# Attention block on one core: the VectorE share of the exponentials by rows of four heads as bit fields and two products, instead of single tiles by a cubic in half precision

## The chip, the cores and the metric

The kernel runs on one core of a Trainium2 chip. The metric is the device time of one execution in microseconds; a measurement is the median of several runs. The core has five engines that run side by side, each through its own list of instructions in order: TensorE (PE, with its weight loads shown apart as PEld), ScalarE (ACT), VectorE (DVE), GpSimd (POOL) and SyncE (SP, which here only starts DMAs). They meet through semaphores. Working memory is SBUF; TensorE writes to PSUM, which has eight banks of 512 fp32 values in each of 128 partitions.

## The reference

One block of multi-head attention, B = 1, S = 2048, D = 448, 16 heads of Dh = 28, all in bf16:

```python
qkv = (x @ wqkv).reshape(B, S, 3, H, Dh).transpose(2, 0, 3, 1, 4)
q, k, v = qkv[0], qkv[1], qkv[2]
scores = jnp.einsum("bhqd,bhkd->bhqk", q, k) * (Dh ** -0.5)
p = softmax(scores, axis=-1)
o = jnp.einsum("bhqk,bhkd->bhqd", p, v)
return o.transpose(0, 2, 1, 3).reshape(B, S, D) @ wo
```

The exponentials are the bulk: 16 x 2048 x 2048 of them. No maximum is subtracted; the row sum is carried by a column of ones in V (column 28 of each head's 32).

## The kernel before

**Tiles and units.** The scores are held transposed: keys on the 128 partitions, 512 queries along the bank. A tile is one head, 128 keys, 512 queries, so one bank. A unit is a group of four heads and a chunk of 512 queries; there are 16 units, and each has 16 key blocks (`kt`) of four tiles, one for each head: 64 tiles a unit, 1024 in all. Below, a *row* is the four tiles of one unit and one `kt`. Scores come out multiplied by 128/ln 2, since Q is scaled so, and ScalarE divides again in its `scale`.

**Two engines take exponentials.** Most tiles go to ScalarE: TensorE writes the scores of a group of tiles to neighbouring banks (line 874, four heads at four row positions of the array, which run side by side), and one ACTIVATE (line 897) turns the whole group into bf16 in `PT`. In unit 0 two groups of two banks take turns (banks 0-1 and 2-3), after it two groups of three (banks 0-2 and 3-5). The other 135 tiles, which a table (`PLAN["tiles"]`) names one by one, go to VectorE through a bank of their own. There, line 919 clips a tile out of PSUM into fp32 `DT`; then two tiles together, 1024 wide, go through lines 931, 933, 935, 937 and 939: a scale of the low 16 bits into fp16, a square, an addition, a product, and a last instruction that adds the polynomial to the fp32 value and rounds it to the 16 bits of a bf16.

**P times V.** For each row, line 830 multiplies the four tiles by V, four heads at four column positions, into one PSUM bank that collects the 16 rows of a unit. This waits for the slowest of the four tiles.

**The rest.** Unit 0 also holds the transposes of x (line 543) and the first projections (560, 577); the other projections of K, Q and V are spread through later units as jobs whose results VectorE moves out of PSUM (lines 529, 531). After a unit, VectorE copies the sum out (line 737), the row sums travel through DRAM to be spread over partitions, and line 753 multiplies by their reciprocals. The last four units also carry the output projection (724, 712). At the end of the last unit a short chain finishes the last 512 queries.

**Banks.** Banks 6 and 7 form the pool "M": the open sum of P times V has one, and the VectorE scores, the projection jobs and the output projection share the other.

**The order.** It is written by a planner in the kernel itself. Each operation has a length, a priority and what it depends on; a list schedule (`schedule`) gives every engine its fixed order. Where TensorE would have too little to do, it inserts passes over zeros (line 479, four matmuls each) that add nothing to an open bank. On the chip an engine that comes to an instruction whose operands aren't there stands, and with it all that is behind it in its list.

The functions follow with the lines of the profile.

Of the kernel before, what the change touches and what calls it, by code (L numbers as in the profile page):

```python
# [7 lines left out]
ALU = mybir.AluOpType  # L8
# [54 lines left out]
class _Prog:  # L63
# [278 lines left out]
PLAN = {
    "tiles": [32, 39, 46, 48, 58, 59, 81, 89, 90, 99, 107, 112, 115, 119, 138, 141, 149, 165, 166, 178, 182, 191, 193, 209, 218, 220, 226, 227, 230, 246, 
# [4 lines left out]
    "late": [0.807, 1.353, 1.300, 1.475, 1.303, 2.070, 1.710, 2.020, 2.419, 2.615, 3.120, 3.693, 4.014, 4.168, 3.895, 4.140, 4.490, 4.389, 4.691, 5.132,   # L348
    5.193, 5.700, 5.935, 5.720, 6.151, 6.521, 6.730, 6.828, 6.866, 6.891, 7.366, 7.749, 7.826, 8.270, 8.397, 8.737, 8.874, 9.279],
# [3 lines left out]
def _fast(nc, x, wqkv, wo, out, n_heads=16):  # L353
# [16 lines left out]
    NPD = 10  # L370
    NDB = 3
# [16 lines left out]
    with es:  # L388
# [3 lines left out]
        x_nat = sb("x_nat", [128, NST, D], BF16)  # L392
# [7 lines left out]
        PD = sb("PD", [128, NPD * 512], I16)  # L400
        DT = sb("DT", [128, NDB, 1024], FP32)
        DW = sb("DW", [128, NDB, 1024], FP16)
        DU = sb("DU", [128, NDB, 1024], FP16)
        OTS = sb("OTS", [128, 2, 512], FP32)
        RS = sb("RS", [128, NU * 16], FP32)
        OTN = sb("OTN", [128, G, S], BF16)
# [1303 lines left out]
```

## Time and profile before

| | |
|---|---|
| median of 3 runs | 418.77 us (418.65 to 418.83) |
| span of the profiled execution | 416.9 us |
| ACT busy | 402.2 us, 96%, 311 instructions |
| DVE busy | 380.1 us, 91%, 615 instructions |
| PE busy | 384.9 us, 92%, 4568 matmuls, of them 1556 over zeros |
| POOL busy | 3.4 us, 9 instructions, all in the first microseconds |
| granted TensorE clock | 1.000 |

The profiled execution is 1.9 us shorter than the median of the runs, since its span goes only from the first to the last instruction. A row of a group gives the line in the code, the engine, the operation with the tile it writes and the tile it reads, their sizes, the count, then the busy time in us and the mean ns of one, and last the idle time before them with what ended it. Busy times of a group are a union: where instructions overlap, the busy time is less than count times mean. The cadence (from one start to the next) is then the better price of an instruction, and it is read from the timeline or from the chain of waits.

### The profile page before, as it was taken

The page shows a single profiled execution, that of the slowest core. Times are in us where ns is not written, and L with a number is a line of the kernel's source. Part 1 is how long each engine was busy: PE and PEld are TensorE (multiplying, and loading weights), DVE is VectorE, ACT ScalarE, POOL GpSimd, SP SyncE. Part 2 cuts the span into 40 slices and gives each one's busy share as a digit, 9 for nine tenths or more (in the row PEclk, how much of TensorE's full clock was granted, in tenths as well). Part 3 has the DMA queues.
Part 4 walks back from the last instruction along what each step waited for, and adds up shares of the span by engine and source line. Part 5 has one row for each costly group of instructions (what it writes and reads, how often), then busy time and mean ns, then how long its engine had stood idle before and what let it go on. Part 6 is the DMA issues. An engine that isn't in the chain of part 4 may idle for free.

```text
span 416.9 us, 10252 instructions
## 1 busy us (share of the span) xinstructions
PE 384.9 (92%) x4568; PEld 122.2 (29%) x4568; DVE 380.1 (91%) x615; ACT 402.2 (96%) x311; POOL 3.4 (1%) x9
## 2 busy tenths in 40 slices
PE   8999989999999999998899899898988999899996
PEld 3432222323332232232232222322223322222223
DVE  6699989999798999999999999999999789999934
ACT  2999999999999999999999999999999999999993
POOL 3000000000000000000000000000000000000000
PEclk9999999999999999999999999999999999999999
DMA  8200000000000000000000000000000000010111
GB/s 264 68 2 3 24 6 7 24 3 28 2 5 27 3 26 2 28 2 8 23 3 30 2 28 2 7 25 3 28 2 28 2 4 27 14 38 24 54 55 57
DMA packets 12982, 10.29 MB, mean 25 GB/s; under 512 B 5064, under 2 KB 10952, under 8 KB 12932
## 3 DMA queue, kind: packets, MB, share of 16 engines
q1 hardware_dynamic: 12132, 8.92, 6.9%
q8 instruction: 37, 0.61, 0.6%
q10 hardware_dynamic: 800, 0.66, 0.5%
q14 instruction: 13, 0.11, 0.1%
HBM read 7.50 MB, written 2.08 MB: 23 GB/s over the span
## 4 chain that ended last, share of the span: by engine, by line
ACT 83%; DVE 7%; DMA 5%; PE 3%; issue 1%; SPq 0%; ACTq 0%
ACT PT L897 83%; DMA RB<-scr_r 2%; DVE DT L919 2%; DMA scr_r<-RS 2%; DMA w_raw<-in_wqkv_dram 1%; DVE PD L939 1%; PE ps L874 1%; DVE DW L931 1%; DVE DU L937 1%; DVE DU L933 1%; PE ps L772 1%; PE ps L830 1%; DVE OTN L753 0%; PE ps L724 0%; DVE OUTS L712 0%
## 5 line engine op out<-in xcount | busy, mean ns | idle before, releaser
L897 ACT ACTIVATE PT<-ps 128x1536 bf16<-128x1536 f32 (+1 forms) x307 | 399.2, 1763 | 1.3 <-PE ps L874 1.0
L874 PE MATMUL ps<-QT,KT 28*128 28x512 bf16 x1024 | 153.2, 384 | 22.9 <-ACT PT L897 18.5
L479 PE MATMUL ps<-ZM,ZW 128*32 128x512 bf16 x1556 | 121.7, 385 | 1.2 <-DVE ZM L461 1.2
L919 DVE TENSOR_SCALAR DT<-ps 128x512 f32<-128x512 f32 x135 | 92.3, 686 | 8.8 <-PE ps L874 8.3
L830 PE MATMUL ps<-PT,V 128*32 128x512 bf16 x889 | 96.1, 388 | 2.6 <-DVE OTS L737 1.0
L874 PEld LDWEIGHTS ps<-QT,KT 28*128 28x128 bf16 x1024 | 36.3, 91 | 157.9 <-ACT PT L897 123.1
L939 DVE SCALAR_TENSOR_TENSOR PD<-DT,DU 128x1024 int16<-128x1024 f32 x68 | 81.9, 1204 | 0.3
L479 PEld LDWEIGHTS ps<-ZM,ZW 128*32 128x32 bf16 x1556 | 37.8, 96 | 39.0 <-issue 20.7
L931 DVE TENSOR_SCALAR DW<-DT 128x1024 f16<-128x1024 uint16 x68 | 46.5, 684 | 0.6
L937 DVE TENSOR_TENSOR DU<-DU,DW 128x1024 f16<-128x1024 f16 x68 | 46.4, 682 | 0.7
L933 DVE TENSOR_TENSOR DU<-DW 128x1024 f16<-128x1024 f16 x68 | 46.3, 681 | 0.6
L830 PE MATMUL ps<-PD,V 128*32 128x512 bf16 x135 | 43.2, 387 | 0.3 <-DVE PD L939 0.2
L830 PEld LDWEIGHTS ps<-PT,V 128*32 128x32 bf16 x889 | 23.7, 93 | 54.9 <-issue 43.6
L560 PE MATMUL ps<-xT,w_raw 112*32 112x512 bf16 x512 | 34.5, 381 | 0.6 <-DMA w_raw<-in_wqkv_dram 0.4
L935 DVE TENSOR_SCALAR DU<-DU 128x1024 f16<-128x1024 f16 x68 | 28.4, 418 | 0.5
L577 PE MATMUL ps<-w_raw,xT 112*128 112x112 bf16 x256 | 16.6, 214 | 0.0
L560 PEld LDWEIGHTS ps<-xT,w_raw 112*32 112x32 bf16 x512 | 11.6, 95 | 14.3 <-issue 2.5
L577 PEld LDWEIGHTS ps<-w_raw,xT 112*128 112x128 bf16 x256 | 13.0, 98 | 5.2 <-issue 4.5
L712 DVE CAST OUTS<-ps 128x448 bf16<-128x448 f32 x14 | 8.5, 622 | 6.0 <-PE ps L724 3.5
L531 DVE CAST KT<-ps 128x512 bf16<-128x512 f32 x16 | 11.0, 687 | 3.2 <-PE ps L560 3.0
L753 DVE TENSOR_TENSOR OTN<-RB,OTS 128x512 bf16<-128x512 f32 x15 | 10.3, 685 | 3.2 <-DMA RB<-scr_r 3.2
L830 PEld LDWEIGHTS ps<-PD,V 128*32 128x32 bf16 x135 | 10.2, 93 | 8.2 <-issue 6.6
(46 smaller groups left out, 94.4 us busy)
## 6 DMA issues: line engine op xcount, KB each, us to landing
RB<-scr_r SPq DMA_DIRECT2D x15, 256.0 KB
out_dram<-OUTS SPq DMA_DIRECT2D x14, 112.0 KB, 1.7
x_nat<-in_x_dram SPq DMA_DIRECT2D x3, 448.0 KB, 7.3
w_raw<-in_wqkv_dram SPq DMA_DIRECT2D x2, 392.0 KB, 6.7
wop<-in_wo_dram SPq DMA_DIRECT2D x16, 24.5 KB
scr_l<-OTS SPq DMA_DIRECT2D x15, 8.0 KB
LT<-scr_l SPq DMA_DIRECT2D x15, 8.0 KB, 1.6
scr_r<-RS SPq DMA_DIRECT2D x15, 8.0 KB, 1.4
```

Source lines behind the costliest of these rows:

```text
L479: ins = e.matmul(ps[32 * h:32 * h + 32, b * 512:(b + 1) * 512], ZW[:, :], ZM[:, :], start=shut, stop=shut, skip_group_check=not shut, tile ...
L560: ins = e.matmul(ps[32 * h:32 * h + 32, b * 512:(b + 1) * 512], w_raw[0:IT, it, col:col + 32], xT[0:IT, it, c * 512:(c + 1) * 512], start= ...
L577: ins = e.matmul(ps[:, b * 512 + j * GD:b * 512 + (j + 1) * GD], xT[0:IT, it, n * 128:(n + 1) * 128], w_raw[0:IT, it, 2 * D + g * GD:2 * D ...
L830: ins = e.matmul(ps[32 * h:32 * h + 32, b * 512:(b + 1) * 512], V[:, kt, hh * 32:(hh + 1) * 32], p_ap, start=(kt == 0), stop=(kt == NK - 1 ...
L874: ins = e.matmul(bank(b), KT[32 * h:32 * h + rows, g, kt * 128:(kt + 1) * 128], QT[32 * h:32 * h + rows, g, c * QCH:(c + 1) * QCH], start= ...
L897: ex = P.add("act", (lambda e, p0=p0, w=w, bf=bf: e.activation(PT[:, p0 * 512:(p0 + w) * 512], bank(bf(), w), AF.Exp, scale=ESCALE)), deps ...
L919: o1 = P.add("dve", (lambda e, T1=T1, s=s: e.tensor_scalar(T1, bank(s.banks[0]), ZLO, ZOFF, ALU.max, ALU.add)), deps=[s, d_last[di]], dur= ...
L931: o2 = P.add("dve", (lambda e, F16=F16, W=W: e.tensor_scalar(W, F16, ES, EC, ALU.mult, ALU.add)), deps=[o for _, o, _ in pair] + [d_last[d ...
L933: o3 = P.add("dve", (lambda e, W=W, U=U: e.tensor_tensor(U, W, W, ALU.mult)), deps=[o2], dur=65 + n * 0.521, prio=pr, name=f"D3_{gi}")
L935: o4 = P.add("dve", (lambda e, U=U: e.tensor_scalar(U, U, EP, None, ALU.add)), deps=[o3], dur=65 + n * 0.261, prio=pr, name=f"D4_{gi}")
L937: o5 = P.add("dve", (lambda e, W=W, U=U: e.tensor_tensor(U, U, W, ALU.mult)), deps=[o4], dur=65 + n * 0.521, prio=pr, name=f"D5_{gi}")
L939: o6 = P.add("dve", (lambda e, U=U, T=T, O=O: e.scalar_tensor_tensor(O, T, ZFIN, U, ALU.add, ALU.add)), deps=[o5] + [slot_last.get(("D", q ...
```

## The change

Four things change together.

**The exponential on VectorE works on rows.** All four tiles of a row go to VectorE or none. Line 886 (of the changed kernel) clips a tile out of PSUM, adds a constant and writes it as a 16-bit integer into `DY`; read as a bf16, that integer is 2^n (1 + f), a first approximation of the exponential. When the four tiles of a row are there, four instructions work on all 2048 elements: line 896 takes the seven fraction bits and puts the exponent of 1 on them, which gives 1 + f as a bf16; line 898 keeps sign and exponent, which gives 2^n (`DS`); line 900 squares 1 + f into fp16 `DU`; line 902 multiplies that square by `DY`, which gives 2^n (1 + f)^3. The exponential is then a sum of three terms, in 2^n (1 + f), 2^n and 2^n (1 + f)^3.

**TensorE adds the terms.** The row's P times V is three passes: `DY` by V, `DS` by V, and `DU` by `VK`, which is V times 0.167. GpSimd makes `VK` with 16 new instructions, one after each V projection (line 577). The passes are queued one by one and wait one by one.

**Which rows.** The table of 135 tiles is gone; a rule over running sums of both engines' work picks 51 rows, 204 tiles: 1 in unit 0, 3 or 4 in each of units 1 to 14, 3 in unit 15. ScalarE keeps 820 tiles. The list of due times for the projection jobs is gone too, and an even spacing takes its place.

**Banks.** After unit 0 the ScalarE groups have three and two banks in turn (0-2 and 3-4), and pool "M" has banks 5, 6 and 7. ScalarE's instructions become 152 of three banks, 181 of two and 2 of one. `x_nat` and `OTN` share storage (`XO`), so line 747 also waits for the transposes of x.

```diff
-    "tiles": [32, 39, 46, 48, 58, 59, 81, 89, 90, ...
-    "late": [0.807, 1.353, 1.300, ...
+    "rows": None,
+    "late": None,
...
-        P.pool("M", [6, 7])
+        P.pool("M", [5, 6, 7])
...
+            vs = V[:, 4 * c:4 * c + 4, g * 128:(g + 1) * 128]
+            vd = VK[:, 4 * c:4 * c + 4, g * 128:(g + 1) * 128]
+            vk_ev[(g, c)] = P.add("pool", (lambda e: e.tensor_scalar(vd, vs, KAP, 1.0, ALU.mult, ALU.mult)), deps=[v_ev[(g, c)]],
...
+            for r in range(NROW):
+                if r % NK == 0:
+                    t_d += dve_load[r // NK]
+                if t_d + CFG["rcost"] <= t_a + CFG["rlead"] and r < NROW - CFG["rend"] and gap >= CFG["rgap"]:
+                    t_d = max(t_d, t_a - 6.0) + CFG["rcost"]
+                    rows.append(r)
+                    gap = 0
+                else:
+                    t_a += 4 * CFG["acost"]
+                    gap += 1
...
-            return ((2, 2), (3, 2), (3, 3))[phase(cur[0])][k % 2]
+            return ((2, 2), (3, 2), (3, 2))[phase(cur[0])][k % 2]
...
+            if r in n_row:
+                ri = n_row[r] % NDR
+                terms = [(V, DY[:, ri, :].bitcast(BF16)), (V, DS[:, ri, :].bitcast(BF16)), (VK, DU[:, ri, :].bitcast(BF16))]
...
+            o1 = P.add("dve", (lambda e, ri=ri, h=h, s=s: e.tensor_scalar(DY[:, ri, h * 512:(h + 1) * 512], bank(s.banks[0]), ZLO, ZADD, ALU.max, ALU.add)),
...
+            og = P.add("dve", (lambda e: e.tensor_scalar(Gt, Y, 0x7F, 0x3F80, ALU.bitwise_and, ALU.bitwise_or)),
+                       deps=row_ops[r] + [old], dur=600, prio=pr, name=f"DG_{r}")
+            os_ = P.add("dve", (lambda e: e.tensor_scalar(S_, Y, 0xFF80, None, ALU.bitwise_and)),
+                        deps=row_ops[r] + [old], dur=600, prio=pr + 0.001, name=f"DS_{r}")
+            ou = P.add("dve", (lambda e: e.tensor_tensor(U, Gt.bitcast(BF16), Gt.bitcast(BF16), ALU.mult)),
+                       deps=[og], dur=1130, prio=pr + 0.002, name=f"DU_{r}")
+            oa = P.add("dve", (lambda e: e.tensor_tensor(U.bitcast(BF16), Y.bitcast(BF16), U, ALU.mult)),
+                       deps=[ou], dur=1130, prio=pr + 0.003, name=f"DA_{r}")
...
-                    o6 = P.add("dve", (lambda e, U=U, T=T, O=O: e.scalar_tensor_tensor(O, T, ZFIN, U, ALU.add, ALU.add)),
```

The planner's order moves with it. First, VectorE's list around the copy of a unit's sum, in the middle of the program. `DT`, `DW`, `DU` and `PD` are the buffers of a pair before; `DY`, `DS` and `DU` those of a row now; `KT` and `QT` are projection results. Before:

```order
L931 TENSOR_SCALAR DW<-DT 128x1024 [waits f_dve]
L919 TENSOR_SCALAR DT<-ps 128x512 [waits f_dve,f_pe]
L933 TENSOR_TENSOR DU<-DW 128x1024 [waits f_dve]
L935 TENSOR_SCALAR DU<-DU 128x1024 [waits f_dve]
L937 TENSOR_TENSOR DU<-DU,DW 128x1024 [waits f_dve]
L531 CAST KT<-ps 128x512 [waits f_pe]
L939 SCALAR_TENSOR_TENSOR PD<-DT,DU 128x1024 [waits f_dve]
L919 TENSOR_SCALAR DT<-ps 128x512 [waits f_pe]
```

Now:

```order
L886 TENSOR_SCALAR DY<-ps 128x512 [waits f_pe]
L896 TENSOR_SCALAR DU<-DY 128x2048 [waits f_dve]
L886 TENSOR_SCALAR DY<-ps 128x512 [waits f_pe] x2
L898 TENSOR_SCALAR DS<-DY 128x2048
L886 TENSOR_SCALAR DY<-ps 128x512 [waits f_pe]
L741 RECIPROCAL RS<-LT 128x16 [waits f_l1]
L900 TENSOR_TENSOR DU<-DU 128x2048 [waits f_dve]
L896 TENSOR_SCALAR DU<-DY 128x2048 [waits f_dve]
L902 TENSOR_TENSOR DU<-DY,DU 128x2048 [waits f_dve]
L519 TENSOR_SCALAR QT<-ps 128x512 [waits f_pe]
```

A pair took seven instructions for two tiles; a row takes eight for four tiles, and the first instruction of the next row stands among the last of this one.

Second, TensorE's list in the middle of the program. 874 (now 864) are scores, 830 (now 832) is P times V, 479 (now 469) the passes over zeros, 560 (now 550) a projection. Before:

```order
L874 MATMUL ps<-QT,KT 128x512 [waits f_act]
L874 MATMUL ps<-QT,KT 128x512 x2
L479 MATMUL ps<-ZM,ZW 32x512 x8
L874 MATMUL ps<-QT,KT 128x512 [waits f_act]
L874 MATMUL ps<-QT,KT 128x512 x2
L830 MATMUL ps<-PT,V 32x512 x4
L560 MATMUL ps<-xT,w_raw 32x512 [waits f_dve]
L560 MATMUL ps<-xT,w_raw 32x512 x15
```

Now:

```order
L864 MATMUL ps<-QT,KT 128x512 [waits f_act]
L864 MATMUL ps<-QT,KT 128x512 x2
L864 MATMUL ps<-QT,KT 128x512 [waits f_act]
L864 MATMUL ps<-QT,KT 128x512
L864 MATMUL ps<-QT,KT 128x512 [waits f_dve]
L832 MATMUL ps<-DU,VK 32x512 [waits f_dve]
L832 MATMUL ps<-DU,VK 32x512 x3
L832 MATMUL ps<-PT,V 32x512 x4
L469 MATMUL ps<-ZM,ZW 32x512 x4
```

Groups of three and of two take turns, a row's third term stands between score groups with a wait for VectorE, and fewer passes over zeros are left: over the whole list 928 matmuls instead of 1556, while P times V goes from 1024 to 1432.

Third, GpSimd's list, which ended with the preparation and now goes on through the units (the last row is new):

```order
L477 MEMSET V 128x256x4
L478 MEMSET V 128x256
L479 MEMSET wop 128x896
L480 MEMSET ONE 128x1
L577 TENSOR_SCALAR VK<-V 128x4x128 x16
```

The 16 instructions on `VK` come one by one, each behind the VectorE copy of the V projection that it reads.

More of the change, by code (lines that the diff above doesn't have):

```diff
@@ L369, in _fast @@
     NPT = 36
-    NPD = 10
-    NDB = 3
+    NDR = 3
     NOB = 4
@@ L679, in _fast @@
             if kind == "A" and b0 is not None:
[L680 to L682 removed]
+                for j in range(b0, b0 + len(idx)):
+                    t_free[j] = gi
         bank_last = {}
@@ L832, in f_pv @@
-                return ins
-            op = P.add("pe", f_pv, deps=list({id(tile_ev[(u, kt, h)]): tile_ev[(u, kt, h)] for h in range(4)}.values())
-                       + [v_ev[(g, kt // 4)]] + (early_ev + mid_ev if kt == 0 and u == 1 else []), acq=((("M" if u else "A"), 1) if kt == 0 else None),
-                       after=[last_pv[0]], kind="c", units=1.0, act=512.0, acc=(True if kt == 0 else False if kt == NK - 1 else None), prio=(u - 60.0 if u == NU - 1 and kt >= NK - 3 else u + (kt + 4) / NK), name=f"PV{u}_{kt}")
@@ L841, in pv @@
+            for s_ in slots:
+                slot_last[s_] = op
+            if r in n_row:
+                row_pv[n_row[r]] = op
             if kt == NK - 1:
@@ L946, in _fast @@
-            if kind == "A":
-                done.update(idx)
+            if pt_pos + w > NPT:
+                pt_pos = 0
+            p0 = pt_pos
+            pt_pos += w
+            s_op = []
+            if b0 is None:
+                bf = (lambda s_op=s_op: s_op[0].banks[0])
+            else:
+                bf = (lambda b0=b0: b0)
+                deps += [bank_last.get(b0 + j) for j in range(w)]
+            s = P.add("pe", (lambda e, tl=tl, bf=bf, s_op=s_op: s_mm(e, tl, range(bf(), bf() + 3), DH, s_op[0].pad)), deps=deps, after=[last_s[0]],
+                      kind="r", units=1.0, act=112.0 * len(tl), heads=tuple(h for _, _, h in tl), prio=-50.0 if b0 is None else pr - 5, name=f"S{gi}",
+                      acq=("M", 1) if b0 is None else None)
@@ new lines, in _fast @@
+            s_op.append(s)
+            last_s[0] = s
+            ex = P.add("act", (lambda e, p0=p0, w=w, bf=bf: e.activation(PT[:, p0 * 512:(p0 + w) * 512], bank(bf(), w), AF.Exp, scale=ESCALE)),
+                       deps=[s] + [slot_last.get(("A", p0 + j)) for j in range(w)], after=[last_exp[0]], dur=52 + w * 427, prio=pr, name=f"E{gi}",
+                       rel=[(s, 0)] if b0 is None else [])
+            last_exp[0] = ex
+            ex.relpool = [("T", b) for b, k_ in t_free.items() if k_ == gi]
@@ new lines, in _fast @@
+            for j, t in enumerate(tl):
+                tile_slot[t] = ("A", p0 + j)
+                tile_ev[t] = ex
+                if b0 is not None:
+                    bank_last[b0 + j] = ex
+            done.update(idx)
+            if todo_rows and 4 * todo_rows[0] - CFG["dlead"] <= idx[-1]:
+                r = todo_rows[0]
+                have = row_heads.setdefault(r, [])
+                free = [h for h in (3, 2, 1, 0) if h not in have and h not in [h_ for _, _, h_ in tl]]
+                for h in free[:int(CFG["nride"]) if ph == 2 else 2]:
+                    have.append(h)
+                    row_tile(r, h, ph, s, pr - 5)
+                if len(have) == 4:
+                    todo_rows.pop(0)
@@ L951, in _fast @@
                 pv_next += 1
+        assert pv_next == NT // 4 and not todo_rows
         ce = None
```

227 lines of the change are left out of this document (90 added, 137 removed), and 4 rows, old and new, of the table PLAN.

## The prediction

> **What bounds the kernel now.** I read the busy times and costliest groups first, then the chain of waits, then the busy time by stretch, and last the timeline.
>
> ```profile
> ACT 83%; DVE 7%; DMA 5%; PE 3%; issue 1%; SPq 0%; ACTq 0%
> L897 ACT ACTIVATE PT<-ps 128x1536 bf16<-128x1536 f32 (+1 forms) x307 | 399.2, 1763 | 1.3 <-PE ps L874 1.0
> L737 DVE COPY OTS<-ps x15: 681/683/692, 38.9 to 384.2; 128x512 f32<-128x512 f32 x15
> 9.66:38.92 29.26, 29.09 (x308) 11.53 (x308) 24.23 (x42) 29.26 (x32) 0.00 (x0) 1.00 0.12 33
> 38.92:384.24 345.32, 320.50 (x3898) 97.60 (x3898) 330.32 (x521) 345.17 (x259) 0.00 (x0) 1.00 0.05 14
> 384.24:416.90 32.66, 27.38 (x269) 9.50 (x266) 19.48 (x42) 25.85 (x22) 0.00 (x0) 1.00 0.17 56
> ```
>
> The second row is the bound: ScalarE's exponentials are 399.2 us busy, and the engine stood 1.3 us in all before them. The last three rows cut the span at VectorE's copies of the first and of the last but one unit's sum (third row); their columns are length, then PE, PEld, DVE, ACT and POOL busy, clock and DMA. In the middle stretch, units 1 to 14, ScalarE works 345.17 of 345.32 us. VectorE works 330.32 and has 15.0 us to spare there. So the kernel ends when ScalarE has done its share, and a tile taken from it is worth something only as long as VectorE can take it: 15 us in 345 is a thin reserve.
>
> **The price of a tile on ScalarE.**
>
> ```profile
> L897 ACT ACTIVATE PT<-ps 128x1536 bf16<-128x1536 f32 x276 | 371.3, 1840 | 0.4 <-PE ps L874 0.2
> L897 ACT ACTIVATE PT<-ps 128x1024 bf16<-128x1024 f32 x30 | 27.7, 1093 | 0.9 <-PE ps L874 0.7
> ```
>
> The records overlap, so the price is busy time by count: 371.3/276 = 1.345 us for three banks, 27.7/30 = 0.923 for two. Three and two in turn cost (1.345 + 0.923)/5 = 0.4536 us a tile, against 0.448 in threes. The changed list has 152 of three, 181 of two and 2 of one (some 0.5 each): 372.5 us, which is 26.7 less than 399.2. **If nothing else bound the kernel, the span would be 416.9 - 26.7 = 390.2 us.** This is the floor.
>
> **The price of a row on VectorE.** The chain of waits runs over VectorE in places; a piece's length there is the time from an instruction's start to the next one's:
>
> ```profile
> 41.60 0.33 DVE DU L935
> 41.93 0.60 DVE DW L931
> 42.53 0.60 DVE DT L919
> 43.13 0.60 DVE DU L937
> 43.73 0.60 DVE DU L933
> 371.37 1.13 DVE PD L939
> ```
>
> Before, a pair costs 2 x 0.60 (clips) + 3 x 0.60 + 0.33 + 1.13 = 4.46, or 2.23 us a tile. How these times grow with width stands in the groups by form, which hold one odd tile of 512:
>
> ```profile
> L937 DVE TENSOR_TENSOR DU<-DU,DW 128x1024 f16<-128x1024 f16 x67 | 46.0, 686 | 0.6
> L935 DVE TENSOR_SCALAR DU<-DU 128x1024 f16<-128x1024 f16 x67 | 28.1, 420 | 0.5
> L937 DVE TENSOR_TENSOR DU<-DU,DW 128x512 f16<-128x512 f16 x1 | 0.4, 424 | 0.0
> L935 DVE TENSOR_SCALAR DU<-DU 128x512 f16<-128x512 f16 x1 | 0.3, 295 | 0.0
> L939 DVE SCALAR_TENSOR_TENSOR PD<-DT,DU 128x1024 int16<-128x1024 f32 x67 | 81.2, 1211 | 0.3
> L939 DVE SCALAR_TENSOR_TENSOR PD<-DT,DU 128x512 int16<-128x512 f32 x1 | 0.7, 692 | 0.0
> ```
>
> A 16-bit product grows by 686 - 424 = 262 ns for 512 elements, so at 2048 it costs 0.60 + 2 x 0.26 = 1.12. The clip still reads 512 fp32 out of PSUM and writes one number for each: 0.60. The two bit-field passes (lines 896 and 898) have no row, since no instruction here does bit operations. Line 935 is nearest in everything else (one 16-bit SBUF source, one 16-bit SBUF result, constants): 420 - 295 = 125 ns for 512, so 0.33 + 2 x 0.125 = 0.58 at 2048. The far bound is the slowest rate here, line 939: 1211 - 692 = 519 ns for 512, so 1.13 + 2 x 0.52 = 2.17. Below 0.58 nothing speaks for. I take 0.58. A row is then 4 x 0.60 + 2 x 0.58 + 2 x 1.12 = 5.80 us, 1.45 a tile.
>
> **So VectorE takes 69 tiles more at almost the same total:** 51 x 5.80 = 296 us against 67.5 pairs x 4.46 = 301. It is relieved of nothing, while ScalarE loses 26.7 us. That turns the bound round, and the sum has to be made by stages.
>
> **The middle stretch, in two halves.** In the changed list (counted between the copies of line 731) all 37 projection copies of this stretch fall into units 1 to 7, none into 8 to 14. Units 1 to 7: 93 clips x 0.60, 45 bit passes x 0.58, 45 products x 1.12, 37 copies at about 0.58 and seven times 1.36 for the work after a unit (0.60 + 0.60 + 0.16): 55.8 + 26.1 + 50.4 + 21.5 + 9.5 = 163.3. Units 8 to 14: 97 clips, 49 passes, 49 products, seven output copies (0.54), the same 9.5: 58.2 + 28.4 + 54.9 + 3.8 + 9.5 = 154.8. The same count with the same prices for the kernel before gives 321 us for this stretch, where the windows show 330.32, so real lists run 2.9% over these prices; I put it on: **168.0 and 159.3 us**. ScalarE has 7 x 64 - 93 = 355 and 448 - 97 = 351 tiles at 0.4536: **161.0 and 159.2 us**. In the first half VectorE is 7 us the slower; in the second the two are equal. VectorE sets the pace: 327.3 us, plus two terms.
>
> *Waits.* VectorE idled 15.0 us here while another engine set the pace. The engine that sets it waits less; but two engines near 100% meet through TensorE's fixed list and lose to each other. Bounds 0 and 15. I take 4, nearer the low end, because VectorE's own longest wait is for scores, and these now share two banks of pool "M" with the projections and not one:
>
> ```profile
> DVE DT L919 <- PE ps L874: 8.3, 12, 2.3
> ```
>
> *The VK work on GpSimd.* It is the first GpSimd work in the middle of the program. What the two engines do to each other shows in the first microseconds:
>
> ```profile
> 1.00 0.95 POOL L487 MEMSET V<- 128x1024 bf16 x1
> 2.01 1.24 POOL L488 MEMSET V<- 128x256 bf16 x1
> 2.06 2.00 DVE L457 CAST id_b<-id_f 128x128 bf16<-128x128 f32 x1
> 2.83 1.16 POOL L489 MEMSET wop<- 128x896 int32 x1
> ```
>
> A 128x128 cast took 2.00 us, until GpSimd's memsets were through; a wider one (512) takes 0.60 elsewhere. So a GpSimd instruction can hold VectorE for about its own length, 1.24 us by the row of a short strided write. Twelve of the 16 fall into the middle stretch, all in its slower half: bounds 0 and 12 x 1.24 = 15 us. I take 3: the clips and copies that read PSUM are almost half of VectorE's time (77 of 163 us), GpSimd can get in beside them, and after a hold the next instructions are ready.
>
> [...]
>
> The middle stretch is then 327.3 + 4 + 3 = 334.3 us, 11.0 less than 345.32. The first and the last stretch lose two ScalarE tiles each (8 clips become 10, 2 become 4): 4 x 0.45 = 1.8. **Span 416.9 - 11.0 - 1.8 = 404.1.** The median of the runs is 418.77 - 416.9 = 1.9 above the span: **406.0 us, 3% faster.**
>
> **What I cost at nothing.** *TensorE's 102 more passes* for the terms:
>
> ```profile
> 366.40 0.33 PE ps L830 x4
> L479 PE MATMUL ps<-ZM,ZW 128*32 128x512 bf16 x1556 | 121.7, 385 | 1.2 <-DVE ZM L461 1.2
> ```
>
> At 0.33 each they are 34 us, and the cover is the zero passes, of which the list drops (1556 - 928)/4 = 157. Without cover, each pass ahead of a score group would hold ScalarE by up to 0.33. *The shared storage XO*: the transposes are over in unit 0, before the first line 747. *The last chain*: the same instructions; one bank from another pool. *Waits for the terms*: `DY` and `DS` passes go ahead of the third, so only that can be late; behind it stand score groups, and through them ScalarE. This is how VectorE sets the pace, and it is in the sum.
>
> **The three-and-two groups.** While ScalarE works on two banks (0.92), TensorE must refill the other three; before, it had 1.35.
>
> ```profile
> 10.00:20.00 10.00, 9.95 (x111) 4.33 (x109) 6.12 (x13) 10.00 (x12) 0.00 (x0) 1.00 0.31 83
> 203.97 4.60 ACT L897 ACTIVATE PT<-ps 128x1536 bf16<-128x1536 f32 x3
> 204.60 0.39 PE L874 MATMUL ps<-QT,KT 28*128 28x512 bf16 x3 [0.19 <-ACT PT L897]
> 205.30 4.61 ACT L897 ACTIVATE PT<-ps 128x1536 bf16<-128x1536 f32 x3
> ```
>
> ACT records start when their scores are there: 0.70 us after the score group's start (204.60 to 205.30). Add some 0.1 to start the group, and the loop is 0.8 us, 0.1 inside the cover. In unit 0, groups of two ran under this same cover, ScalarE busy 10.00 of 10.00 us. I take nothing, and keep the other end as a rival.
>
> **The rivals.**
> - *ScalarE stays the bound* (chance 0.20): VectorE's 2.9% surplus was waiting that goes away (then 318 us of work in the middle stretch, under ScalarE's 320) and VK costs nothing. For it: ScalarE hides all of that in the kernel before. Against it: the first half, 163 to 161 even at bare prices. Span 390 to 394, time 392 to 396.
> - *VK takes the shared ports in full* (0.12): 15 in place of 3, and the time is 418.0; with half of it, some 411. For it: the cast of 2.00 us. Against it: almost half of VectorE's time is in PSUM reads. [...]
> - *The three-bank refill is late* (0.09). A pass of P times V or a late third term just ahead of the score group takes the 0.1 us that is left. One pass of 0.33 before each of the 152 three-bank groups is up to 152 x 0.33 = 50 us on the floor of 392: 442. It decides from (418.8 - 392)/152 = 0.18 us a group on; above that the kernel is slower. For it: the after-list puts terms there. Against it: unit 0.
> - *The bit passes run at the slow rate* (0.05): 102 x (2.17 - 0.58) = 162 us on VectorE, about 565. The gain of 12.8 is gone already at 0.58 + 12.8/102 = 0.71 us a pass.
> - *Nothing moves* (0.04): the terms above add to 13, within 0.2% of the time before (0.2%, 0.8 us, is about what a measurement of this kernel can tell from no change).
>
> **How the numbers follow.** My case, VectorE setting the pace between 398 and 411, has 0.50. Faster: 0.50 + 0.20 + 0.12 = 0.82; same 0.04; slower 0.14. The range goes from the floor (390.2 + 1.9, rounded down to 391) to VK's full price, 418; it leaves out the slower cases and a little below.
>
> **What would show it.** Right, if the after-profile has DVE busy at 375 us or more in a span near 404 and ScalarE with idle time in units 1 to 7 above all, ended by TensorE's scores. The bit passes show in their mean (some 0.66 us recorded), the products near 1.2, two-bank groups at 0.92 of busy time each. VK shows in bit passes or products far above their mean where GpSimd is busy. I am wrong if ScalarE is still without idle time, if it idles evenly over all units with VectorE idle as well (then it is the refill), or if the bit passes take over 0.8 us.

## The result, and the profile after

| | before | changed |
|---|---|---|
| median | 418.71 us (418.50 to 418.83) | 401.7 us (398.51 to 408.48) |
| ratio to before, 95% interval | | 0.957 (0.951 to 0.962) |
| predicted | | 406.0 us (391 to 418) |

The changed kernel is 4.3% faster, where 3% was forecast. The ratio leaves out the slowest execution, 408.48 us, which counts as slow (over 1.5% above the fastest); the median has it in. The times spread over 10 us, and the spread follows the mean granted clock of TensorE (executions sorted by span):

| execution of the changed kernel | 1 | 2 | 3 | 4 |
|---|---|---|---|---|
| mean granted clock | 1.000 | 0.996 | 0.983 | 0.970 |
| span, us | 396.7 | 397.7 | 402.1 | 406.7 |

That is some 3.3 us for each hundredth. The kernel before is not free of this: 38 executions of it beside the experiments had clocks of 0.992 to 1.000 and times of 418.4 to 422.5 us. Below, a span of another kernel is compared with this table at the same clock, read between its columns where need be, and to about 1 us: executions of one kernel at one clock differed by that much. The profiled execution is the fourth one, so its page must be read with the clock beside it. Busy times and clock by slice, the chain of waits and the groups:

```profile
PE 386.9 (95%) x4331; PEld 123.9 (30%) x4331; DVE 371.8 (91%) x548; ACT 378.0 (93%) x339; POOL 16.8 (4%) x25
PEclk9999969999999999999999999999999957999999
ACT 43%; DVE 34%; PE 19%; DMA 2%; issue 1%; SPq 0%
L939 ACT ACTIVATE PT<-ps 128x1536 bf16<-128x1536 f32 (+1 forms) x335 | 375.0, 1317 | 14.6 <-PE ps L864 13.9
L886 DVE TENSOR_SCALAR DY<-ps 128x512 int16<-128x512 f32 x204 | 132.7, 679 | 11.0 <-PE ps L864 10.8
L902 DVE TENSOR_TENSOR DU<-DY,DU 128x2048 bf16<-128x2048 bf16 x51 | 61.9, 1213 | 0.1
L896 DVE TENSOR_SCALAR DU<-DY 128x2048 int16<-128x2048 int16 x51 | 34.7, 680 | 0.3
L898 DVE TENSOR_SCALAR DS<-DY 128x2048 int16<-128x2048 int16 x51 | 34.6, 678 | 0.0
L577 POOL TENSOR_SCALAR VK<-V 128x512 bf16<-128x512 bf16 x16 | 13.4, 837 | 171.6 <-DVE V L521 171.6
```

The chain that was 83% ScalarE and 7% VectorE is now shared, 43 and 34, with 19% on TensorE. ScalarE's exponentials fell from 399.2 to 375.0 us (372.5 was forecast), and they wait for scores, 13.9 us against 1.0. The clock row shows two places where TensorE lost speed, in units 1 and 13; more than half of ScalarE's waits, and a part of TensorE's share of the chain, lie there. Between them the clock is 1.00. The windows, cut as those of before (length, then PE, PEld, DVE, ACT and POOL busy, clock, DMA share and GB/s):

```profile
40.83:376.80 335.97, 322.42 (x3638) 98.45 (x3639) 323.75 (x466) 323.89 (x284) 10.54 (x12) 0.96 0.05 15
67.23:210.90 143.67, 140.17 (x1667) 47.74 (x1664) 143.63 (x210) 141.34 (x125) 9.93 (x11) 1.00 0.05 14
210.90:322.65 111.75, 104.18 (x1250) 29.17 (x1250) 110.37 (x157) 110.95 (x99) 0.00 (x0) 1.00 0.05 15
```

The first row is the whole middle stretch, units 1 to 14. The second and third are the parts of it at full clock, units 2 to 7 and 8 to 12. In units 2 to 7 VectorE works 143.63 of 143.67 us, and ScalarE stands 2.3. In units 8 to 12 both are within 1.4 us of the whole window. TensorE has 3.5 and 7.6 us left. So the change turned a kernel with one full engine into one with two, and a third close behind them.

### The profile page after: what moved, and what is told of

The parts are those of the page before. It is cut to its first block, busy times and chain, and to the rows that moved or that the text cites. A ratio compares the mean times of both kernels' runs of the same rounds, so it can differ in the third digit from the quotient of the medians.

```text
span 406.7 us, 9742 instructions
## 1 busy us (share of the span) xinstructions
PE 386.9 (95%) x4331; PEld 123.9 (30%) x4331; DVE 371.8 (91%) x548; ACT 378.0 (93%) x339; POOL 16.8 (4%) x25
## 4 chain that ended last, share of the span: by engine, by line
ACT 43%; DVE 34%; PE 19%; DMA 2%; issue 1%; SPq 0%
ACT PT L939 43%; DVE DY L886 11%; PE ps L864 7%; DVE DU L900 6%; DVE DU L902 5%; PE ps L832 5%; DVE DU L896 3%; DVE DS L898 3%; PE ps L469 3%; PE ps L718 2%; DMA LT<-scr_l 2%; PE ps L550 2%; DVE V L521 1%; DVE KT L521 1%; DVE QT L519 1%; DVE OTS L731 1%
## 5 line engine op out<-in xcount | busy, mean ns | idle before, releaser
L939 ACT ACTIVATE PT<-ps 128x1536 bf16<-128x1536 f32 (+1 forms) x335 | 375.0, 1317 | 14.6 <-PE ps L864 13.9
L886 DVE TENSOR_SCALAR DY<-ps 128x512 int16<-128x512 f32 x204 | 132.7, 679 | 11.0 <-PE ps L864 10.8
L469 PE MATMUL ps<-ZM,ZW 128*32 128x512 bf16 x928 | 74.9, 399 | 1.2 <-DVE ZM L451 1.2
L902 DVE TENSOR_TENSOR DU<-DY,DU 128x2048 bf16<-128x2048 bf16 x51 | 61.9, 1213 | 0.1
L900 DVE TENSOR_TENSOR DU<-DU 128x2048 f16<-128x2048 bf16 x51 | 61.8, 1213 | 0.0
L896 DVE TENSOR_SCALAR DU<-DY 128x2048 int16<-128x2048 int16 x51 | 34.7, 680 | 0.3
L898 DVE TENSOR_SCALAR DS<-DY 128x2048 int16<-128x2048 int16 x51 | 34.6, 678 | 0.0
L832 PE MATMUL ps<-DU,VK 128*32 128x512 bf16 x204 | 20.8, 397 | 0.0
L832 PE MATMUL ps<-DY,V 128*32 128x512 bf16 x204 | 20.8, 397 | 0.0
L832 PE MATMUL ps<-DS,V 128*32 128x512 bf16 x204 | 20.6, 394 | 0.0
L577 POOL TENSOR_SCALAR VK<-V 128x512 bf16<-128x512 bf16 x16 | 13.4, 837 | 171.6 <-DVE V L521 171.6
```

What stands on the lines that cost most here:

```text
L469: ins = e.matmul(ps[32 * h:32 * h + 32, b * 512:(b + 1) * 512], ZW[:, :], ZM[:, :], start=shut, stop=shut, skip_group_check=not shut, tile ...
L832: ins = e.matmul(ps[32 * h:32 * h + 32, b * 512:(b + 1) * 512], w_[:, kt, hh * 32:(hh + 1) * 32], p_[h], start=(kt == 0 and k == 0), stop= ...
L886: o1 = P.add("dve", (lambda e, ri=ri, h=h, s=s: e.tensor_scalar(DY[:, ri, h * 512:(h + 1) * 512], bank(s.banks[0]), ZLO, ZADD, ALU.max, AL ...
L896: og = P.add("dve", (lambda e: e.tensor_scalar(Gt, Y, 0x7F, 0x3F80, ALU.bitwise_and, ALU.bitwise_or)), deps=row_ops[r] + [old], dur=600, p ...
L898: os_ = P.add("dve", (lambda e: e.tensor_scalar(S_, Y, 0xFF80, None, ALU.bitwise_and)), deps=row_ops[r] + [old], dur=600, prio=pr + 0.001, ...
L900: ou = P.add("dve", (lambda e: e.tensor_tensor(U, Gt.bitcast(BF16), Gt.bitcast(BF16), ALU.mult)), deps=[og], dur=1130, prio=pr + 0.002, na ...
```

## The experiments

Each run was measured beside the kernel before. Where the expectations give a list's number of zero passes (792 to 1960), they count matmuls over zeros, as the profile does. In the planner a pass is four of them. Their "full clock" is the mean granted clock of 1.000.

### Is VectorE the bound, or ScalarE? Half of VectorE's wide work

The four wide instructions of a row work on 1024 elements and not 2048; half of the row's work on bit fields and products is left out, and the terms of heads 2 and 3 are read from those of heads 0 and 1.

```diff
...
-            Y, S_, U = DY[:, ri, :], DS[:, ri, :], DU[:, ri, :]
+            Y, S_, U = DY[:, ri, 0:1024], DS[:, ri, 0:1024], DU[:, ri, 0:1024]
```

> The changed kernel with the four wide VectorE instructions of a row on 1024 elements instead of 2048; the second and third terms of heads 2 and 3 use those of heads 0 and 1, so half of the row's work is left out. Same instructions, same order, same waits. A row costs 4 x 0.60 + 2 x 0.33 + 2 x 0.60 = 4.26 us in place of 5.80, 79 us less on VectorE. Theory A (at full clock VectorE sets the pace of the changed kernel): the span falls from 396.7 to the ScalarE floor, 390 to 392, time 392 to 394, and VectorE stands idle for some 70 us. Theory B (ScalarE with its groups of three and two, or the order of TensorE's list, sets the pace): the span stays within 1.5 us of 396.7 in executions at full clock.

Measured: 397.6 us (397.1 to 402.1), ratio 0.950 (0.944 to 0.957). Spans of 395.3 to 396.3 at 0.996 stand against 397.7. The busy times, ScalarE's group, and the middle stretch:

```profile
PE 372.7 (94%) x4331; PEld 119.8 (30%) x4331; DVE 301.0 (76%) x548; ACT 376.2 (95%) x339; POOL 14.7 (4%) x25
L940 ACT ACTIVATE PT<-ps 128x1536 bf16<-128x1536 f32 (+1 forms) x335 | 373.2, 1325 | 5.4 <-PE ps L865 5.1
40.14:366.07 325.93, 308.91 (x3638) 95.07 (x3636) 259.18 (x465) 322.25 (x285) 8.66 (x12) 0.99 0.05 16
```

VectorE lost 71 us of work and the kernel 1.4 to 2.4 us. Behind VectorE stands ScalarE, 322.25 of 325.93 us busy. The prediction had put 14 us between VectorE's pace and ScalarE's floor, and theory A goes by that; theory B, within 1.5 us, is much the nearer.

### One row more, fewer rows

The planner's price of a row, 5.6 us, is changed, and it picks another number of rows (shown for the first of four):

```diff
-CFG = {... "rcost": 5.6, ...}
+CFG = {... "rcost": 5.4, ...}
```

> The planner's price for a row on VectorE goes from 5.6 to 5.4 us; it then takes 52 rows and not 51 (208 tiles), with 876 zero passes and not 928. ScalarE's theory (ScalarE sets the pace, VectorE has a few us to spare): four tiles fewer on ScalarE at 0.4536 us are -1.8 us, span at full clock about 395, median 397 to 401 with the clock as it falls. The prediction's theory (VectorE sets the pace): one row more is +5.8 us on VectorE, of which units 2 to 12 carry most; span at full clock 400 to 402, median 404 to 407. TensorE's list: 52 fewer zero passes at 0.046 us each would take another 2.4 us off.

> The planner's price for a row goes from 5.6 to 5.9 us; it then takes 48 rows and not 51 (192 tiles), with 1048 zero passes and not 928. ScalarE's theory: twelve tiles more on ScalarE at 0.4536 us are +5.4 us: span at full clock about 402, and by TensorE's list 120 more zero passes at 0.046 us add up to 5.5 us more, about 407. The prediction's theory (VectorE sets the pace): three rows of 5.8 us less on VectorE, the time falls until ScalarE binds, 390.2 + 5.4 = 395.6, so a span of 395 to 397 at full clock: the same as the changed kernel or 1 us faster.

The 52 rows took 412.9 us (ratio 0.983, 0.978 to 0.988), 48 rows 409.1 (0.977, 0.970 to 0.983). At equal clock that is some 8 us slower on both sides (410.1 at 0.982 against 402.4; 405.4 at 1.000 against 396.7). ScalarE's forecast missed the first and, with TensorE's zeros added, held for the second (402 to 407). The prediction's theory missed both: the first in size, 4 to 5 us slower in place of 8, the second in sign. Part of the first was an accident of its end: 16.3 us from the last exponential to the end of the span, where the changed kernel has 7.8. Hence two more runs, with prices of 5.45 and 5.7 that keep the changed kernel's last seven rows:

> 52 rows again, by a planner's price of 5.45 us a row: here the last seven rows (223 to 251) are those of the changed kernel, so that the end of the program is not planned anew as it was in the first run with 52 rows, whose last exponential ended 16.3 us before the end of its span and not 7.8 as in the changed kernel. 792 zero passes and not 928. If VectorE and ScalarE stand within 2 us of each other at 51 rows, one row more (5.8 us on VectorE) puts VectorE ahead: span at full clock 400 to 403, VectorE busy in all of units 2 to 12 and ScalarE idle there for 4 us or more. If ScalarE paces alone: 396.7 - 1.8 = 395, and 6 us less if TensorE's zero passes pace. If the first run's 12 us were all of its end, this run comes back to 395 to 397.

> 50 rows by a planner's price of 5.7 us, again with the last seven rows of the changed kernel (223 to 251), 968 zero passes. If VectorE and ScalarE stand close at 51 rows, ScalarE paces here: four tiles more at 0.4536 us are +1.8 us, span at full clock 398 to 399, VectorE with 4 us or more to spare in units 2 to 12. If VectorE paced by the margin that the prediction gave it (14 us of span over ScalarE's floor), one row less would take 4 us off at least: 392 to 393. If the zero passes pace, 40 more are +1.8 us and this adds to ScalarE's: 400 to 401.

| rows on VectorE | zero matmuls | span at a mean clock | the changed kernel at that clock |
|---|---|---|---|
| 48 | 1048 | 405.4 at 1.000 | 396.7 |
| 50 | 968 | 405.2 at 0.992 | 399.1 |
| 51 (changed) | 928 | | 396.7 at 1.000 |
| 52, second list | 792 | 400.7 at 0.993 and at 0.996 | 398.7 and 397.7 |
| 52, first list | 876 | 410.1 at 0.982 | 402.4 |

The medians of the new two were 403.7 us (ratio 0.964, 0.960 to 0.968) and 408.6 (0.976, 0.972 to 0.981). The middle stretches of 52 rows (second list) and of 48, both at full clock:

```profile
40.99:368.15 327.16, 313.72 (x3528) 96.63 (x3531) 326.35 (x471) 324.93 (x286) 13.83 (x12) 1.00 0.05 16
43.30:374.90 331.60, 314.30 (x3706) 98.69 (x3702) 315.57 (x444) 327.44 (x289) 12.69 (x12) 1.00 0.05 16
```

With 52 rows VectorE stands 0.8 us in 327.2 and ScalarE 2.2, so VectorE paces, though ScalarE's idle time is less than the 4 us that was expected. With 48 VectorE has 16 us to spare, ScalarE 4.2, and the stretch is 4 us longer. By these busy times 51 rows stand near the meeting point: VectorE paces just above it, and well below it VectorE does not. The spans alone do not show it, since the number of zeros changes with the rows: at the price measured below (some 0.05 us a matmul) 48 rows pay 6 us for zeros, and the second list of 52 saves 7. The 50 rows fit in sign; their 6 us are more than four tiles (1.8) and 40 zero matmuls (2.0) explain, and each number of rows is also a newly planned list, in which an engine may stand for other reasons (TensorE once stood 2.48 us there, ended by nothing that the profile shows). That remainder is open.

### The end of the program with 52 rows

The second list lost its time after the last exponential. The clock of the profiled execution fell only in the last 6 us, in which TensorE has nothing to do, so its 400.7 us can be held against the 396.7 at full clock. ScalarE's last rows, and VectorE's:

```profile
371.35 14.15 ACT L939 ACTIVATE PT<-ps 128x1536 bf16<-128x1536 f32 x13 [0.18 <-PE ps L864]
393.18 0.54 ACT L704 ACTIVATE OUTS<-ps 128x448 bf16<-128x448 f32 x1 [7.67 <-DMA out_dram<-OUTS]
```

```profile
390.78 2.14 DVE L706 CAST OUTS<-ps 128x448 bf16<-128x448 f32 x3
395.45 1.16 DVE L706 CAST OUTS<-ps 128x448 bf16<-128x448 f32 x2 [2.53 <-issue]
397.84 0.62 DVE L706 CAST OUTS<-ps 128x448 bf16<-128x448 f32 x1 [1.23 <-DMA out_dram<-OUTS]
```

The exponentials end at 385.5, the span at 400.7; in the changed kernel these are 398.9 and 406.7. So the end is 15.2 us and not 7.8. Three output copies of unit 14 stand behind the whole chain of unit 15, and four output buffers make the copies wait for DMAs. A further run puts that in order:

```diff
-    NOB = 4
+    NOB = 8
...
-  ... dur=610, prio=pr + 0.2, name=f"NM{u}", slack=CFG["nslack"])
+  ... dur=610, prio=pr + 0.2 - (60.0 if u == NU - 2 else 0.0), name=f"NM{u}", slack=CFG["nslack"] if u < NU - 2 else 0.0)
...
-                    out_proj(c * NQT + j, pr + 0.2 * j, "dve")
+                    out_proj(c * NQT + j, pr + 0.2 * j - (50.0 if u == NU - 2 else 0.0), "dve")
```

> The second run with 52 rows, with the end of the program put in order: the normalisation of unit 14 and its four output projections go ahead of the last unit's work (priorities, and no slack behind the DMA of its reciprocals), and eight output buffers instead of four. In the run before it the last exponential ended at 385.5 and the span at 400.7: 15.2 us of end, in which unit 14's three last output copies stood behind the last unit's and waited for output buffers; in the changed kernel the last exponential ended at 398.9 of 406.7, 7.8 us of end. Theory that the body gained from the 52nd row and only the end lost: end of 8 to 9.5 us, span 394 to 395 at the clock of that run (0.993), 396 to 397 us, about 1 us less at full clock, and a median 4 to 6 us under the changed kernel's 401.7. Rival, that VectorE's 5.8 us more come back at the end whatever its order (the row's products are late for the last exponential's groups, or unit 14's output copies delay the last unit's): 399 to 403, as before it. Granted clock 0.985 to 1.000 in either case.

Measured: 400.9 us (400.0 to 402.8), ratio 0.955 (0.952 to 0.958); 398.3 at 0.996 to 0.998, against 400.7 before the repair and 397.7 for the changed kernel, all near 0.996. Of the 3 to 4 us by which the second list was behind, 2.4 came back; the time lies in the rival's range, 399 to 403, and not 4 to 6 us under the changed kernel's:

```profile
386.01 2.85 ACT L939 ACTIVATE PT<-ps 128x1536 bf16<-128x1536 f32 x3 [0.82 <-PE ps L864]
394.52 0.62 DVE L706 CAST OUTS<-ps 128x448 bf16<-128x448 f32 x1
397.83 0.62 DVE L706 CAST OUTS<-ps 128x448 bf16<-128x448 f32 x1 [2.69 <-issue]
```

From the last exponential (388.9) to the end of the span (400.8) are 11.9 us, not the 8 to 9.5 expected: two copies still come last, and ahead of the very last VectorE stands 2.69 us, ended by nothing that the profile shows. The median is 0.8 us below the changed kernel's, with intervals that overlap; no version was found that clearly beats it.

### GpSimd's share

The 16 GpSimd instructions are left out, and the third term takes V; the scaling by 0.167 is so left out.

```diff
...
-            vk_ev[(g, c)] = P.add("pool", (lambda e: e.tensor_scalar(vd, vs, KAP, 1.0, ALU.mult, ALU.mult)), deps=[v_ev[(g, c)]],
-                                  dur=1500, prio=prio, name=f"vk_{g}_{c}")
+            vk_ev[(g, c)] = v_ev[(g, c)]
...
```

> The changed kernel without GpSimd's 16 instructions on VK; the third term is multiplied by V, so the scaling by 0.167 is left out. The prediction's term (GpSimd holds VectorE): 3 us less at full clock (span 394), up to 10 (13.4 us of GpSimd work recorded). Rival (the holds lie beside VectorE's PSUM reads or are taken up by slack): no difference at full clock, spans of 396 to 398.

Measured: 398.0 us (397.5 to 404.2), ratio 0.947 (0.944 to 0.951). Three executions at full clock had spans of 395.8 to 396.2, against 396.7: VK costs less than 1 us, which is about what spans at one clock differ by, not 3, and not 15. The mean of VectorE's products shows nothing of it:

```profile
L899 DVE TENSOR_TENSOR DU<-DY,DU 128x2048 bf16<-128x2048 bf16 x51 | 62.1, 1217 | 0.1
```

That is 1217 ns without any GpSimd work beside it, 1213 with it.

### The banks and the exponential, each alone

First the old exponential with its table of 135 tiles and the new banks; then the new exponential with the old banks.

```diff
-        P.pool("M", [6, 7])
+        P.pool("M", [5, 6, 7])
...
-            return ((2, 2), (3, 2), (3, 3))[phase(cur[0])][k % 2]
+            return ((2, 2), (3, 2), (3, 2))[phase(cur[0])][k % 2]
```

> The kernel before with the changed banks alone: groups of three and two, pool M with banks 5, 6 and 7; the old exponential with its 135 tiles and its table. If the gain is all the exponential's: groups of two cost 889 x 0.0053 = 4.7 us, so 423 us, or 419 to 424. If the banks carry part of the gain (VectorE's scores no longer wait for the one bank of M): under 417.5.

```diff
-        P.pool("M", [5, 6, 7])
+        P.pool("M", [6, 7])
...
-            return ((2, 2), (3, 2), (3, 2))[phase(cur[0])][k % 2]
+            return ((2, 2), (3, 2), (3, 3))[phase(cur[0])][k % 2]
```

> The edit keeps the new exponential, its three terms and 51 rows, and gives the banks back as they were before: six banks for the score groups (three and three), two for the other products. It fills the fourth corner beside the kernel before, the kernel with the old exponential and the new banks (428.99) and the changed kernel (401.7). Theory that exponential and banks add up: the banks alone cost 8 to 9 us there, so without them the new exponential should give 401.7 - 9 = about 393 us. Rival, that the exponential needs the third bank: three terms a tile hold the product banks longer, score groups then meet a list that the planner has to fill with 1960 zero passes where the changed kernel has 928; by the run with 304 more zero passes (14 us slower at full clock, 0.046 us each) the 1032 more would cost up to 47 us: about 430 to 450, slower than before, with TensorE the busiest and ScalarE idle over 40 us.

Measured: 429.0 us (428.2 to 430.4), ratio 1.022 (1.017 to 1.027), and 486.8 us (484.1 to 491.8), ratio 1.157 (1.149 to 1.166). The banks alone cost 9 us, the exponential alone 68, and both together save 17. In the first, the groups of three and two make ScalarE 5.4 us busier than before (402.2 there), and VectorE's 381.3 us are those of before:

```profile
PE 404.2 (94%) x4749; PEld 129.8 (30%) x4749; DVE 381.3 (89%) x615; ACT 407.6 (95%) x366; POOL 3.4 (1%) x9
```

That is ScalarE's part of the price, and the forecast of 419 to 424 us had that part alone. This list also has 1744 zeros, where the one before has 1556; how the rest of the price divides is not shown. Of the run with the new exponential and the old banks, busy times and two rows of the waits (total, times, longest):

```profile
PE 449.5 (92%) x5401; PEld 148.2 (30%) x5401; DVE 383.3 (78%) x548; ACT 374.0 (76%) x288; POOL 22.8 (5%) x25
ACT PT L939 <- PE ps L864: 85.6, 28, 11.5
DVE DY L886 <- PE ps L864: 64.8, 80, 2.8
```

With a single bank beside the open sum, VectorE's clips wait for their scores 80 times, 64.8 us; ScalarE waits 85.6 us in 28 pieces of up to 11.5; and the planner puts 1960 matmuls over zeros into the list. The loss came out still larger than the rival theory's 430 to 450. Its executions also ran at clocks of 0.959 to 0.986. The sign is clear; how it divides between the bank, the zeros and the clock is not. The even spacing of the projection jobs goes with the new exponential in these runs and was not run alone.

### TensorE: zeros and the clock

Thresholds of the rule that inserts zeros were raised, twice:

```diff
-    FILL_MUST = 3750.0
-    FILL_HOT = 2787.5
+    FILL_MUST = 4250.0
+    FILL_HOT = 3400.0
...
-CFG = {... "hotm": 3600.0, ...}
+CFG = {... "hotm": 4000.0, ...}
```

> The changed kernel with the planner asked for more passes over zeros: 1232 zero matmuls instead of 928, everything else by the same rules. Theory (the spread of the changed kernel's times is the TensorE clock: it was granted in full in the 396.7 us execution and at 0.970 in the 406.7 us one): the clock is 1.000 in every execution, the spans lie within 1.5 us of each other and near 397, the median time near 399. Rival (the clock dips only mark stretches in which TensorE waits for something else): the spread stays, and 76 more passes of 0.22 us, some of them ahead of score groups, add up to 17 us to the fastest span, so 405 to 413.

The second run has 3950, 3000 and 3800 there.

> The rule that fills TensorE's list with zero passes gets thresholds between those of the changed kernel and of the run with 1232 (an earlier run, 14 us slower at full clock): 1056 zero passes, 128 more than the changed kernel; rows and banks as there. If the cost is in proportion, 128 x 0.046 = 6 us: span at full clock 402 to 403. If zero passes cost only where they stand ahead of score groups that ScalarE waits for, a smaller number costs less than its share, 397 to 400. As to the clock: if the gate closes where TensorE's list is thin, the dips become rarer and the spread of the mean clock narrows to 0.99 to 1.00 (more than the 0.970 to 1.000 of the changed kernel); if it closes at the stop near the middle of the program, the spread stays.

Measured: 417.2 us (413.0 to 418.0), ratio 0.992 (0.988 to 0.995), for 1232 matmuls over zeros; 405.4 us (405.4 to 406.9), ratio 0.968 (0.965 to 0.971), for 1056. At full clock the spans are 411.1 and 403.6, against 396.7 with 928: 14.4 and 6.9 us, 0.047 and 0.054 us a matmul. The first lies in its rival's 405 to 413, the second just above the 402 to 403 of a cost in proportion. So TensorE's list is close to full as well. With 1232, ScalarE's waits for scores grow to 20.9 us, nearly 5 of them at a stop and a stretch of half clock shown at the end of this document:

```profile
L939 ACT ACTIVATE PT<-ps 128x1536 bf16<-128x1536 f32 (+1 forms) x335 | 376.5, 1263 | 22.0 <-PE ps L864 20.9
```

On the clock the runs do not agree. With 1056 the four mean clocks were 0.996 to 1.000, with 1232 the ten were 0.988 to 1.000, where the theory had 1.000 in all. One more run took up a place in the changed kernel where TensorE's list is thin, just ahead of the second dip:

```profile
312.00:322.00 10.00, 9.28 (x113) 2.32 (x105) 10.00 (x15) 10.00 (x10) 0.00 (x0) 1.00 0.05 18
323.00:324.00 1.00, 0.39 (x4) 0.00 (x0) 1.00 (x3) 1.00 (x2) 0.00 (x0) 1.00 0.00 0
326.00:330.00 4.00, 4.00 (x28) 0.73 (x20) 2.54 (x4) 2.16 (x3) 0.00 (x0) 0.50 0.02 2
342.00:346.00 4.00, 4.00 (x35) 1.23 (x32) 3.89 (x6) 4.00 (x4) 0.00 (x0) 1.00 0.04 14
```

TensorE is 0.39 busy in one microsecond, and from 324 on its clock is 0.50, until about 341, though from 325 on it is busy all that time; the other two engines then work little more than half of theirs. At that place TensorE has closed the sum of unit 12, which VectorE copies at 322.65, and its list has no matmuls over zeros from 321.7 to 325.1. The edit moves the last row of four units, 3, 7, 9 and 13, by one:

```diff
-    "rows": None,
+    "rows": [14, 21, ..., 59, 62, 69, ..., 123, 126, 133, ..., 155, 158, 164, ..., 219, 222, 229, ...],
```

> The edit moves four rows of the VectorE table by one: rows 63, 127, 159 and 223, the last row groups of their units, become 62, 126, 158 and 222; 51 rows and 204 tiles as before. Theory of the thin place: in the profiled changed kernel the granted clock falls to 0.50 behind the end of unit 13, where the order gives TensorE only score groups and pads for about 3 us while VectorE works on row 223; with the row one earlier TensorE gets real products there, the dip behind unit 13 vanishes from the profile (the granted clock stays above 0.9 between 310 and 345 us), and more executions come near a span of 396.7 at a mean clock of 1.000: median 399 or less, the largest less than 402. Rival: the gate closes at whatever stretch happens to be thin in that execution (the stretch of 47 to 58 us and the stop near 230 us are others); then the spread stays at 398.5 to 408 and dips show at other places. By the rows nothing else should move: span at full clock 396 to 398.

```profile
202.00:203.00 1.00, 0.99 (x14) 0.21 (x12) 1.00 (x3) 1.00 (x2) 0.00 (x0) 0.98 0.00 0
204.00:217.00 13.00, 13.00 (x93) 2.35 (x87) 9.66 (x13) 9.55 (x8) 0.00 (x0) 0.51 0.01 3
310.00:345.00 35.00, 33.34 (x382) 9.32 (x375) 34.51 (x49) 35.00 (x32) 0.00 (x0) 1.00 0.06 21
```

The expectation takes the thin place for the end of unit 13, with row 223. By the trace of the changed kernel it is the end of unit 12: 41 rows, up to row 204, have been multiplied by then, and row 223's last term comes at 352.84. So the edit puts no products there. The list planned anew has 28 matmuls over zeros there instead (from 322.4 to 325.3), and TensorE is at least 0.8 busy in each microsecond from 318 to 332. The dip is gone from that place in the profiled execution. Another came at 203, where TensorE had been 0.75 busy in one microsecond and 0.88 to 0.99 in the three after it. The median is 401.1 us (398.8 to 403.5), ratio 0.954 (0.946 to 0.961), the spans 397.0 at 0.998 and 401.5 at 0.982, on the table of the changed kernel. So a thin place went away, but that did not keep the clock up; the rival holds. Where the dips fall is known for one execution of each kernel alone. What brings the clock down is open.

## Why the prediction was right, and where not

**The turn of the bound.** Right in direction, too large in size. It said VectorE the slower in the first half, by 7 us, the two equal in the second; the windows show 143.63 against 141.34 us and 110.37 against 110.95. But with half of its wide work gone the kernel gained 2.4 us at most, where the sum had VectorE 14 us above ScalarE's floor. Of the signs that it named, ScalarE's idle time came, ended by scores and mostly in the first units (2.3 us, then 0.8); VectorE's 375 us did not, it was busy 371.8.

**The price of a row.** Right: 5.80 us was forecast. VectorE's timeline in the changed kernel gives it from start to start:

```profile
371.60 0.68 DVE L896 TENSOR_SCALAR DU<-DY 128x2048 int16<-128x2048 int16 x1
372.20 1.28 DVE L886 TENSOR_SCALAR DY<-ps 128x512 int16<-128x512 f32 x2
373.40 0.68 DVE L898 TENSOR_SCALAR DS<-DY 128x2048 int16<-128x2048 int16 x1
374.00 0.68 DVE L886 TENSOR_SCALAR DY<-ps 128x512 int16<-128x512 f32 x1
374.60 1.21 DVE L900 TENSOR_TENSOR DU<-DU 128x2048 f16<-128x2048 bf16 x1
375.73 1.15 DVE L706 CAST OUTS<-ps 128x448 bf16<-128x448 f32 x2
```

Clips 0.60, bit passes 0.60 (0.58 forecast), products 1.13 (1.12): 5.86 us. The rival of slow bit passes fell.

**The middle stretch, 334.3 us, was 8 us too long.** This is the step that failed, in size: the surcharge, the waits and VK. The span at full clock, 396.7, less the first and last stretch of the profiled execution (40.83 and 29.90) leaves 326.0; that assumes that these two stretches run as there. The bare sum for VectorE was 163.3 + 154.8 = 318.1. On it were put 9.2 us of a 2.9% surcharge, 4 of waits and 3 of VK. In the run with 52 rows, where VectorE does set the pace, the instructions of that stretch (197 clips, 95 bit passes, 95 products and 37, 5 and 14 of the rest) come to 322.9 us at the prediction's prices, and VectorE is 326.35 busy and 0.8 idle: 1.1%, and hardly a wait; with the bit passes at 0.60 and the products at 1.13 the instructions come to 325.7. With 48 rows, where VectorE idles 16.0 us, the same count comes to 303.6 us, and it is 315.57 busy: 3.9%. So the surcharge goes with idle time, of which the kernel before had 15.0 us. The records show how: that of a clip is 0.68 us long, while the next instruction can start after 0.60, so busy time grows where nothing follows at once. To put 2.9% and then waits on an engine that sets the pace was too much on both counts. VK was less than 1.

**Where the rest of the stretch is.** VectorE at 1.1% would be 322 us and ScalarE's floor is 320.2, but the stretch takes 326.0. With VectorE relieved it still took 325.93, at 0.996. A part of this is that the bound changes with the units. In units 2 to 12 VectorE's instructions, at the measured 0.60 and 1.13, come to 254.4 of 255.4 us. In units 1, 13 and 14, which take the other 70.6, they come to 67.7, and ScalarE's 152 tiles at 0.4536 to 68.9; in the run with half of the work ScalarE is busy 46.86 of 47.25 us in units 13 and 14. The larger one in each part makes 323.3 us, and some 3 us are lost by neither engine's work. ScalarE waits for scores (5.4 us of idle before its group in the run with half of the work), and more zeros lengthen the program. That points to TensorE's list, which the prediction had costed at nothing. No run took zeros away and left the rows as they are, so this stays open.

**Costed at nothing.** The 102 passes for the terms were covered as forecast: with 157 zero passes gone TensorE's busy time went from 384.9 to 386.9 us, the latter at the lower clock (the same matmuls took 372.7 in the run with half of VectorE's work, at 0.996). But the cover was not spare; 32 passes put back cost 6.9 us. The three-and-two handoff was free: in units 8 to 12 ScalarE stands 0.8 us over 99 instructions, 0.008 us each, where that rival needed 0.18 to decide.

**The ends.** 40.83 + 29.90 = 70.7 us against 71.6: 0.9 less, and 1.8 was forecast. Each was to lose 0.9; the last lost 2.8, and the first grew by 1.9, which no run explains.

**The rivals.** *ScalarE stays the bound* comes closest in size, since the span of 396.7 lies 6.5 us above its floor, but it is wrong that VectorE then has time left: one row more is slower. *VK in full* fell: less than 1 us in place of 15. No run shows the shared ports that it is named after. With 13.4 us of VK in the program the products' mean is 1213 ns, and 1217 without. In the trace of the changed kernel seven wide products (lines 900 and 902) stand partly beside VK, six of them 1.21 to 1.26 us long and one 1.63; one line 747 took 1.10 us there, where the median is 0.68. The clips and copies out of PSUM beside VK took 0.67 to 0.68 us.

**Not foreseen: the clock.** Nothing in the profile before, at 1.000 throughout, spoke of it. It adds nothing to the best execution and 10 us to the worst, and the median span stands 3.2 us above the one at full clock. The forecast of 406.0 is thus 4.3 us high as the difference of two misses: 7.4 us too much in the sum (8.3 in the middle stretch, less 0.9 in the ends), and 3.2 us of clock that was not in it; the last 0.1 is the step from span to time, 1.8 us and not 1.9. That the two partly cancel is luck: at full clock the time was 398.5 us, a gain of 20.2 where 12.8 was forecast.

## What to carry to other kernels

When work is moved until a second engine fills, take the bare sum of each engine for each stage and let the larger one decide; a surcharge read off an engine that had time to spare goes with its idle time (3.9% with 16.0 us idle, 1.1% with 0.8), and shrinks when it sets the pace. Here the bare sums give 163.3 + 159.2 = 322.5 us for the middle stretch, 3.5 short, where the forecast was 8.3 long. A table that splits work between two engines is to be tried one step to both sides, and the end of the program looked at each time: here one row more, with 136 zeros fewer, brought the last exponential forward by some 3 us and made what follows it 7 us longer, and still 4 after the repair. When a profile shows three engines above 90%, look for what the third one's list still holds, since "covered" there is not "spare".

## What the runs showed of the hardware

- The granted clock of TensorE halved for 7 to 17 us at a time (0.50 from 51 to 57 and from 324 to about 341 us in one execution), while TensorE was busy nearly throughout. The places differ between kernels: behind a microsecond at 0.39 busy, behind one at 0.75 and three at 0.88 to 0.99, and, with 1232 matmuls over zeros, behind a stop of 3.52 us that nothing in the profile ends. What lowers the clock and what brings it back is not shown:

```profile
237.27 0.40 PE L832 MATMUL ps<-PT,V 128*32 128x512 bf16 x4 [3.52 <-issue]
238.00:246.00 8.00, 8.00 (x71) 1.62 (x67) 6.51 (x9) 5.97 (x5) 0.00 (x0) 0.57 0.01 2
```

- A 16-bit integer bit operation on 2048 elements took VectorE 0.60 us from start to start, as long as a clip of 512 fp32 values out of PSUM.
- Sixteen GpSimd instructions of 0.84 us, most of them beside a full VectorE, cost less than 1 us in all.
